# Who writes a block of ones: a memset moved from VectorE to GpSimd at the start of an attention kernel

## The chip, the cores and the metric

The kernel runs on 1 core of one Trainium2 chip. The metric is device time in microseconds (us), the median over the executions. Most executions agree within 0.3%. An execution that is over 1.5% above the fastest of its kernel is classed as slow, and the ratios below use fast executions alone.

## The reference, cut to what matters

```
a   = softmax(phi, axis=seq)                       # 8 batches, 8 heads, 576 tokens, 32 memories
k_m = a^T k ;  v_m = a^T v                         # sums over the tokens
y   = softmax(q k_m^T / 8) v_m                     # attention over the memories
out = ((x @ w_a) * (x @ w_b)) @ w_out              # x: the heads of y side by side
```

The softmax over tokens is never normalised first. The kernel multiplies exp(phi) into k, v and a block of ones beside them; the product with the ones is the denominator. The block holds 1/16 and not 1, which is the scaling that float16 wants here. It is the "fill" of this study. There is one for each of two buffers, and it is written once per buffer.

## The kernel before: the parts that matter

```python
kv_sbs = [consts.tile([P, 3, NHP, NI * D], F16, name=f"kv_sb{t}") for t in range(2)]
#                         ^ plane 0: k, plane 1: v, plane 2: the fill
...
k_f32 = ht[:, 0:2].bitcast(F32)
nc.scalar.dma_start(out=k_f32, in_=rows(k, 0)[:, 0:2])   # half of k, as float32, ScalarE's queue
load_phi(0)                                              # SyncE's queue
load_q(0, halves[0]); load_k(0, halves[1])               # from here GpSimd's queue
load_q(0, halves[1]); load_v(0)
...
make_identity(nc, ident)                                 # GpSimd: a memset and a select
nc.vector.memset(kv_sbs[0][:, 2], 1.0 / CS)              # the fill, L155
nc.vector.tensor_copy(out=kvs[0][:, 0, 0:2], in_=k_f32)  # cast of k, L156
load_wab(0, 256)                                         # weights, GpSimd's queue
ones = ...                  # another tile, not the fill: VectorE memset, two GpSimd selects
load_wab(256, 512); load_wab(512, 1024); load_wab(1024, 1536)
load_wo(0); load_phi(1); ...
nc.gpsimd.memset(kv_sbs[1][:, 2], 1.0 / CS)              # the second buffer's fill, much later
```

TensorE's first real work (L256, "the first sums") reads exp(phi), the cast half of k and the fill. Some 23 us later comes "the last fold" (L337): the product of v_m with the last third of the weights w_b. Both are landmarks below.

## Time and profile before

| | before |
|---|---|
| time, median of 3 | 247.86 us (247.41 to 247.93) |
| span of the profiled execution | 246.2 us |
| first sums start | 7.74 us |
| last fold starts | 30.66 us |
| TensorE busy, over the whole span | 95% |

A busy share of 95% says that TensorE bounds the kernel as a whole. It does not say what bounds the first 30 us. The prediction shows the page's main lines and those of the start. One place it did not look at is the end of the start. Here are the last two folds in the timeline of TensorE (start, duration, engine, line, operation, count, and in brackets the idle time before it and who ended it).

```profile
30.10 0.41 PE L337 MATMUL pva<-wa_sb,kvT 64*32 64x512 f16 x8
...
30.66 0.11 PEld L337 LDWEIGHTS <-kvT 64*32 64x32 f16 x8 [0.45 <-DMA wb_sb<-in_moe_w_b_dram]
30.66 0.41 PE L337 MATMUL pva<-wb_sb,kvT 64*32 64x512 f16 x8 [0.15 <-ACT a_sb L587]
```

The matmul's row has a wait of 0.15 us, and names ScalarE. A reader of that row alone would say that the transfers are no issue. But the weight load that starts with it (PEld) had waited 0.45 us, and for wb: its last part was issued at 14.30 and took 16.3 us to land, so it came near 30.6, just before the fold. TensorE was ready only a little sooner. So already in this profile the stream of loads holds the last fold.

### The profile page before, as it was taken

The page shows a single profiled execution, that of the slowest core. Times are in us where ns is not written, and L with a number is a line of the kernel's source. Part 1 is how long each engine was busy: PE and PEld are TensorE (multiplying, and loading weights), DVE is VectorE, ACT ScalarE, POOL GpSimd, SP SyncE. Part 2 cuts the span into 40 slices and gives each one's busy share as a digit, 9 for nine tenths or more (in the row PEclk, how much of TensorE's full clock was granted, in tenths as well). Part 3 has the DMA queues.
Part 4 walks back from the last instruction along what each step waited for, and adds up shares of the span by engine and source line. Part 5 has one row for each costly group of instructions (what it writes and reads, how often), then busy time and mean ns, then how long its engine had stood idle before and what let it go on. Part 6 is the DMA issues. An engine that isn't in the chain of part 4 may idle for free.

```text
span 246.2 us, 7624 instructions
## 1 busy us (share of the span) xinstructions
PE 233.1 (95%) x3016; PEld 165.7 (67%) x3016; DVE 168.6 (68%) x405; ACT 158.6 (64%) x410; POOL 152.8 (62%) x124
## 2 busy tenths in 40 slices
PE   7589999999998999999999999999999999999992
PEld 2334574456665857777787777877787878888881
DVE  3454784468959968876994559865996586756651
ACT  2364772678697489578856768587856867465430
POOL 8734263499799028892899759892849087946000
PEclk9855999999999999999999999999999999999999
DMA  6999999999969804973159832696120303033253
GB/s 202 209 197 207 209 254 206 256 217 284 225 174 209 165 3 105 235 134 88 27 137 216 184 85 44 160 201 160 35 53 3 85 12 77 19 72 75 45 129 95
DMA packets 26035, 33.81 MB, mean 137 GB/s; under 512 B 1936, under 2 KB 20368, under 8 KB 26000
## 3 DMA queue, kind: packets, MB, share of 16 engines
q0 software_dynamic: 19280, 22.71, 50.5%
q1 hardware_dynamic: 6368, 9.97, 16.3%
q10 hardware_dynamic: 352, 0.66, 0.7%
q8 instruction: 23, 0.38, 0.6%
q14 instruction: 12, 0.10, 0.1%
HBM read 42.47 MB, written 9.44 MB: 211 GB/s over the span
## 4 chain that ended last, share of the span: by engine, by line
PE 89%; DVE 3%; DMA 3%; ACT 2%; issue 1%; DVEq 0%
PE pa L584 21%; PE pb L594 19%; PE py L462 16%; PE pv L462 8%; PE pva L337 6%; PE po L389 5%; PE px L462 4%; DMA phi_sb<-in_phi_dram 3%; PE pkv L213 2%; PE pD L314 2%; PE pscore L292 2%; PE pk L256 2%; PE pT L274 1%; PE pT L242 1%; ACT a_sb L587 1%
## 5 line engine op out<-in xcount | busy, mean ns | idle before, releaser
L597 DVE TENSOR_TENSOR ht<-a_sb,pb 128x288 f16<-128x288 f16 x192 | 83.0, 449 | 41.9 <-ACT a_sb L587 28.7
L587 ACT CAST a_sb<-pa 128x288 f16<-128x288 f32 x192 | 75.0, 406 | 31.6 <-PE pa L584 29.3
L584 PE MATMUL pa<-A,vab 128*128 128x288 f16 x384 | 77.4, 291 | 1.6 <-DVE A L325 1.1
L594 PE MATMUL pb<-A,vab 128*128 128x288 f16 x384 | 77.2, 289 | 0.7 <-ACT vab L349 0.5
L444 POOL TENSOR_TENSOR h_sums<-ht 128x768 f16<-128x768 f16 x28 | 45.8, 1639 | 38.8 <-DVE ht L597 37.3
L594 PEld LDWEIGHTS <-vab 128*128 128x128 f16 x384 | 37.5, 99 | 13.4 <-issue 1.7
L584 PEld LDWEIGHTS <-vab 128*128 128x128 f16 x384 | 34.9, 99 | 16.1 <-issue 8.7
L462 PEld LDWEIGHTS <-h_sums 128*128 128x128 f16 x384 | 37.4, 98 | 6.9 <-issue 0.4
L349 ACT CAST vab<-pva 128x512 f16<-128x512 f32 (+1 forms) x52 | 28.0, 559 | 12.0 <-PE pva L337 12.0
L349 DVE CAST vab<-pva 128x512 f16<-128x512 f32 (+1 forms) x52 | 32.6, 643 | 2.9 <-PE pva L337 2.2
L462 PEld LDWEIGHTS <-ht 128*128 128x128 f16 x288 | 28.1, 98 | 5.6 <-issue 0.4
L462 PE MATMUL py<-w_sums,h_sums 128*128 128x256 f16 x192 | 30.3, 272 | 0.0
L444 POOL TENSOR_TENSOR h_sums<-h_sums,ht 128x768 f16<-128x768 f16 x14 | 23.1, 1647 | 1.0
L444 POOL TENSOR_TENSOR h_sums<-ht,h_sums 128x768 f16<-128x768 f16 x14 | 23.0, 1640 | 1.0
L305 ACT ACTIVATE E<-pscore 128x288 f16<-128x288 f32 x32 | 11.4, 417 | 11.3 <-PE pscore L292 11.2
L325 POOL TENSOR_TENSOR A<-E,R 128x576 f16<-128x576 f16 x10 | 12.8, 1275 | 7.1 <-ACT R L323 6.8
L462 PE MATMUL py<-wo_sb,ht 128*128 128x256 f16 x96 | 16.0, 273 | 0.0
L462 PE MATMUL pv<-w_sums,h_sums 128*128 128x256 f16 x96 | 16.0, 272 | 0.0
L469 ACT ACTIVATE u<-py 128x256 f32<-128x256 f32 x32 | 12.4, 387 | 5.2 <-PE py L462 5.0
L462 PE MATMUL py<-w_sums,ht 128*128 128x256 f16 x96 | 15.5, 272 | 0.1
L462 PE MATMUL px<-wo_sb,ht 128*128 128x256 f16 x96 | 15.4, 273 | 0.0
L204 DVE STREAM_TRANSPOSE qT<-q_sb 128x288 f32<-128x288 f32 x32 | 14.3, 462 | 0.6 <-DMA q_sb<-in_q_dram 0.6
(62 smaller groups left out, 262.7 us busy)
## 6 DMA issues: line engine op xcount, KB each, us to landing
out_dram<-o_sb SPq DMA_DIRECT2D x70, 128.0 KB, 2.6
kv_sb<-in_v_dram POOLq DMA_DIRECT2D x7, 576.0 KB, 10.4
phi_sb<-in_phi_dram POOLq DMA_DIRECT2D x7, 576.0 KB, 4.7
kv_sb<-in_k_dram POOLq DMA_DIRECT2D x7, 576.0 KB, 8.2
q_sb<-in_q_dram POOLq DMA_DIRECT2D x6, 576.0 KB, 13.4
wo_sb<-in_moe_w_out_dram POOLq DMA_DIRECT2D x3, 512.0 KB, 16.3
q_sb<-in_q_dram POOLq DMA_DIRECT2D x4, 288.0 KB, 12.6
wa_sb<-in_moe_w_a_dram POOLq DMA_DIRECT2D x2, 512.0 KB, 14.9
```

The costliest lines, as they stand in the source:

```text
L204: nc.vector.transpose(out=t["qT"][:, hp, :].bitcast(F32), in_=qs[b][:, hp, :].bitcast(F32))
L325: engine.tensor_tensor(out=attn[b][:, g, sl], in0=t["E"][:, g, sl], in1=t["R", g][:, sl], op=ALU.mult)
L337: nc.tensor.matmul(t["pva", lo, z][g][0][32 * j:32 * j + 32, 0:hi - lo], t["kvT"][64 * r:64 * r + 64, 4 + g, M * j:M * j + M], w_sbs[z][64 ...
L349: engine_copy(out=vabs[b][z][:, g, lo:hi], in_=pva[:, 0:hi - lo])
L389: nc.tensor.matmul(po, ht[:, i, P * c:P * (c + 1)], wo_sb[:, i, :], start=(i == 0), stop=(i == NFF - 1))
L444: engine.tensor_tensor(out=out, in0=in0, in1=in1, op=op)
L462: nc.tensor.matmul(po, lhs[:, i], rhs[:, i], start=first and i == 0, stop=i == KH - 1, skip_group_check=not first)
L469: nc.scalar.mul(out=x, in_=po, mul=scale)
L584: nc.tensor.matmul(pa, vab[0][:, g, fs], A[:, g, HALF * hf:HALF * (hf + 1)], start=(g == 0), stop=(g == 1))
L587: nc.scalar.copy(out=a_sb, in_=pa)
L594: nc.tensor.matmul(pb, vab[1][:, g, fs], A[:, g, HALF * hf:HALF * (hf + 1)], start=(g == 0), stop=(g == 1))
L597: nc.vector.tensor_tensor(out=ht[:, i, t0:t0 + HALF], in0=a_sbs[hf - hfs[0]], in1=pb, op=ALU.mult)
```

## The change

The fill goes to GpSimd. It stays in its place in program order, which on GpSimd is behind the first four loads and the identity, and ahead of the weight loads. The intent is to take 2 us from VectorE at the start.

```diff
     make_identity(nc, ident)
-    nc.vector.memset(kv_sbs[0][:, 2], 1.0 / CS)
+    nc.gpsimd.memset(kv_sbs[0][:, 2], 1.0 / CS)
     nc.vector.tensor_copy(out=kvs[0][:, 0, 0:2], in_=k_f32)
     load_wab(0, 256)
```

> **What bounds the kernel now.** I read the page from the top: the busy table, then the clock row, then the chain of work that ended last.
>
> ```profile
> PE 233.1 (95%) x3016; PEld 165.7 (67%) x3016; DVE 168.6 (68%) x405; ACT 158.6 (64%) x410; POOL 152.8 (62%) x124
> PEclk9855999999999999999999999999999999999999
> PE 89%; DVE 3%; DMA 3%; ACT 2%; issue 1%; DVEq 0%
> ```
>
> TensorE is the bound over the span of 246.2 us: 95% busy and 89% of the chain. The clock row dips in slices 2 to 4 only, so the start is the one stage where TensorE waits for others and runs slowly. The change touches only the start. I therefore took the chain of waits for the first 10 us (columns: start in us, duration, what).
>
> ```profile
> 0.81 6.17 DMA phi_sb<-in_phi_dram
> 6.98 0.02 issue
> 7.00 0.69 ACT exp_sb L195
> 7.70 0.04 issue
> 7.74 0.71 PE pk L256 x36
> ```
>
> The start hangs on one transfer. phi of batch 0, issued by SyncE at 0.81, lands at 6.98; ScalarE's exponential follows; the first real matmuls start at 7.74. Those matmuls (the sums of k and of the ones for one half of the heads) also read the fill of ones, so 7.74 is the deadline that matters for the fill. No memset is on the chain. The timeline of the first 8 us shows who is busy before the deadline (start, duration, engine, line, operation, output and input, count, idle before it and its releaser).
>
> ```profile
> 1.32 0.89 POOL L90 DMA_DIRECT2D q_sb<-in_q_dram  x1 [0.80 <-POOLq L699]
> 1.63 1.98 DVE L155 MEMSET kv_sb<- 128x2304 f16 x1 [0.43 <-issue]
> 2.20 0.72 POOL L82 DMA_DIRECT2D kv_sb<-in_k_dram  x1
> ...
> 3.63 0.77 POOL L85 DMA_DIRECT2D kv_sb<-in_v_dram  x1
> ...
> 4.68 0.29 POOL masks.py:199 TENSOR_SCALAR_AFFINE_SELECT ident<-ident 128x128 f16<-128x128 f16 x1
> 4.93 0.77 POOL L99 DMA_DIRECT2D wa_sb<-in_moe_w_a_dram  x1
> ...
> 6.63 0.76 DVE L156 CAST kv_sb<-ht 128x1152 f16<-128x1152 f32 x1 [3.02 <-DMA ht<-in_k_dram]
> ```
>
> VectorE finishes the fill at 3.61 and then stands idle for 3.02 us until k lands; so taking the fill from it buys nothing by itself. GpSimd is free of its four issues and of the identity at 4.97, and from there it queues the weight loads.
>
> **What the Trainium skill says.** On the page "SBUF — State Buffer", section "Who interferes with whom", a VectorE instruction with at most one SBUF input and outside the two-port modes does not contend with GpSimd; copies and casts in SBUF can enter a two-port mode, and then whichever of the two engines starts first holds the shared ports and the other blocks fully. The first half agrees with the trace as far as the issue rows tell: the issues at 2.20 and 3.63, beside the memset, took 0.72 and 0.77, like the 0.77 of the one at 4.93, which has no VectorE work beside it. That two such operations can block each other at all also shows here: the product of E and R (two SBUF inputs) took 1480 ns at 73.63 beside a GpSimd sum that reads SBUF, against a median of 459 ns.
>
> "DMA: Bandwidth & Descriptors", section "SWDGE vs HWDGE vs iDMA", says that GpSimd writes its descriptors into rings in SBUF while loads from SyncE and ScalarE do not use that path, and that the two kinds feed different queues between which a DMA engine takes turns. The queue view of 0.5 us windows (packets, MB, share of 16 engines) shows the first GpSimd packets surprisingly late:
>
> ```profile
> q10 hardware_dynamic: 60, 0.14, 69.8%
> q1 hardware_dynamic: 58, 0.07, 37.0%
> ...
> q1 hardware_dynamic: 100, 0.11, 62.2%
> q10 hardware_dynamic: 43, 0.08, 39.5%
> q0 software_dynamic: 3, 0.00, 4.0%
> ```
>
> Above is 4.5 to 5.0, below 5.0 to 5.5. The first packet of q0, GpSimd's queue, comes about 5.4, 4.1 us after the first issue at 1.32. At 125.81, where the queue was empty, it took about 1.3 us. Either the two hardware queues, which fill the engines (37.0 + 69.8% = 107%), hold q0 back, or the descriptors come late. This is the doubtful point of the case; I return to it under the rivals.
>
> "TensorE: Matmul & The Clock Gate", Part 1, puts the clock down to activity in free-running windows of 3413 ns. The trace agrees in kind: the windows view has a granted clock of 1.00 over 7 to 10 us, 0.56 over 10 to 17, 0.54 over 17 to 25, and 1.00 after that.
>
> **The change part by part.** Removed: one VectorE memset of 1.98 us. Value on the path: 0, because what follows it on VectorE waited 3.02 us for a transfer.
>
> Added: one GpSimd memset of the same 128x2304 f16. The kernel has exactly this instruction already, for the second buffer, and its row says 2.04 us at 34.26. It stands behind the identity, so it runs from 4.68 + 0.29 = 4.97 to 4.97 + 2.04 = 7.01. The first reader started at 7.74 and was released at 7.70. Slack: 7.70 - 7.01 = 0.69 us. Path cost: 0.
>
> Moved: everything that GpSimd does later. The loads of wa and wb for columns 0 to 256 go from 4.93 and 5.68 to about 6.97 and 7.72. The two selects that make the block of ones go from 7.61 to about 8.5 and end near 9.1, while the denominators, their reader, begin at 12.91: 3.8 us of slack. The next four weight loads, 0.75 each, go from 8.25-11.23 to about 9.1-12.2; the load after them had waited until 11.48 for q and now issues about 12.2, and the next one waits for v at 14.30 as before. There the delay has been absorbed.
>
> Do later issues make later data? Only if the queue runs dry. The first four loads bring 288 + 288 + 288 + 576 KB, 1.47 MB, at some 0.2 MB/us from 5.4 on: the queue has its own work until 5.4 + 7.4 = about 12.8 (v lands at 3.63 + 10.4 = 14.0), and the packets indeed turn small, as the weights' are, near 12.5 (224 packets in the 12th us, 360 in the 13th). The weights must be queued by then; issued at 6.97 they have five microseconds in hand. So weights land unchanged. Path cost: 0.
>
> Contention, the one term that is not zero. The VectorE cast of k, at 6.63, is an SBUF-to-SBUF copy: 1152 elements in 761 ns is 1.5 elements/ns, well above one per cycle of a 0.96 GHz engine (clock from "VectorE: DVE Perf Modes", "Specifications"), so it very likely runs in a two-port mode. The new memset still holds the ports until 7.01. If the lock applies to a memset, which only writes, the cast waits 7.01 - 6.63 = 0.38 us and ends at 7.39 + 0.38 = 7.77 and not 7.39. The matmuls need it too and would start about 0.04 us later, near 7.81, and not at 7.74: +0.07 us. Add up to 0.05 us if TensorE now has to pass one more semaphore. Sum: 0 + 0 + 0 + 0.07 + some 0.03 = +0.1 us, an estimate from these rows, and it reaches the end undiminished at most, since TensorE is the bound nearly throughout.
>
> **The rivals.** (1) The old memset did hold up GpSimd's descriptors, in spite of the rule. For it: q0 starts 4.1 us after its issue and not 1.3, and only after the memset is over. Then q0 would start perhaps 2 us sooner, near 3.4, while the transfers of phi and k fill the engines. Early q is worth nothing, as q is not on the chain; phi is. Some 0.9 MB of phi and k are outstanding at 3.4; if q0 takes a third of the engines, an arithmetic estimate is up to 0.9/0.39 x 0.5 = 1.2 us later, more likely 0.5 to 1. Result about 248.3 to 248.9. Against it: the issue rows show no lengthening, and full engines explain the wait as well. I give it 20%.
>
> (2) The fill is late: GpSimd memsets or the four issues take longer beside each other, and TensorE waits on the fill. It would have to lose over 0.69 us; the row at 34.26 ran beside VectorE work and the issues have no reason to slow. It would make +0.3 us or so. 10%.
>
> (3) It helps: GpSimd not writing weight descriptors from 4.93 to 6.4 frees phi and k, or the freed VectorE lets something start sooner. Nothing on the chain waits for that; -0.2 us at best. 10%.
>
> (4) The clock: a shift of the matmuls against the activity windows may move the dip by a window of 3.4 us; at half clock that might be worth up to about 1 us either way, although the three runs of before, whose phases need not agree, lie within 0.52 us.
>
> **Range and chances.** 247.86 + 0.1 = 247.96, say 248.0 us. Downwards, rivals 3 and 4 and the scatter (247.41 to 247.93) give 247.2; upwards, rivals 1 and 4 give 248.8. A 2% change is 5 us, which none of the terms or rivals comes near: faster 0.01, same 0.98, slower 0.01.
>
> **What would show it.** Right: the memset on GpSimd's timeline at about 4.97 for 2.0 us; phi landing still at about 7.0; q0's first packets still near 5.4; the first weight load issued near 7.0 but the fold's first matmuls not later than some 0.1 us; the cast of k ending near 7.8 (lock) or 7.4 (none). Wrong: q0's packets from about 3.4 and phi landing well after 7 (rival 1); the first sums released by the GpSimd memset (rival 2); a clock dip of another length (rival 4). A time under 246 or over 250 would mean a mechanism that I have not seen.

## The result, and the profile after

| | before | after |
|---|---|---|
| time, median of 4 | 247.90 us (247.41 to 247.94) | 247.84 us (247.59 to 248.32) |
| ratio of fast runs | | 1.0007, 95% interval 0.9993 to 1.0021 |
| span of the profiled execution | 246.2 us | 245.8 us |
| first sums start | 7.74 us | 7.71 us |
| last fold starts | 30.66 us | 30.29 us |

A ratio is the mean time of one kernel's fast runs over that of the other's of the same rounds, so it is not quite the ratio of the medians. The verdict is: the same. The interval, some -0.2 to +0.5 us, holds both zero and the predicted +0.1 us.

The timeline of the changed kernel between 4 and 10 us, in the same columns:

```profile
4.93 2.01 POOL L155 MEMSET kv_sb<- 128x2304 f16 x1
...
6.57 0.99 DVE L156 CAST kv_sb<-ht 128x1152 f16<-128x1152 f32 x1 [5.37 <-DMA ht<-in_k_dram]
6.89 0.97 POOL L99 DMA_DIRECT2D wa_sb<-in_moe_w_a_dram  x1
6.93 1.26 ACT L195 ACTIVATE exp_sb<-phi_sb 128x576 f16<-128x576 f32 x2 [4.31 <-DMA phi_sb<-in_phi_dram]
...
7.71 0.68 PE L256 MATMUL pk<-kv_sb,exp_sb 64*32 64x128 f16 x36 [0.88 <-DVE ones L160]
```

The fill runs from 4.93 to 6.94. VectorE's idle time ahead of the cast grows from 3.02 to 5.37 us: the freed time went straight into waiting for k. The cast takes 0.99 and not 0.76, and the first weight load is issued at 6.89 and not 4.93; beside the cast its issue takes 0.97 and not 0.77. The first sums still start 0.78 us after the exponential (6.93 to 7.71), against 0.74 before (7.00 to 7.74).

GpSimd's queue, q0, still sends its first packets in the window from 5.0 to 5.5 us (packets, MB, share of the engines; 3 packets and 4.0% before):

```profile
q0 software_dynamic: 4, 0.00, 5.3%
```

Two rows of the page look as if the start had changed its nature:

```profile
PEclk9977999999999999999999999999999999999998
...
PE 82%; DMA 11%; DVE 3%; issue 1%; ACT 1%; POOL 1%; DVEq 0%; POOLq 0%
```

The clock dip is shallower, and the chain that ended last is now 11% transfers against 3%. The chain itself (start, duration, what) says why:

```profile
3.63 10.32 DMA kv_sb<-in_v_dram
13.94 0.28 issue
14.23 16.02 DMA wb_sb<-in_moe_w_b_dram
30.24 0.04 issue
30.29 0.41 PE pva L337 x8
```

In this execution TensorE was quicker through the start (its fold before the last began at 28.90, against 30.10) and stood waiting at the last fold, 0.97 us by its timeline row, until the last part of wb had landed at 30.24. In the kernel before wb landed near 30.6 and the fold followed at once too. The chain of the page followed the matmul's row there, and so ScalarE: the step from 3% to 11% is a near-tie that fell the other way, and no change in the start's nature. From the last fold to the end the two profiles take the same time: 246.2 - 30.66 = 215.5 us before and 245.8 - 30.29 = 215.5 us after. So the 0.4 us between the spans lies wholly before the last fold, and a floor that no memset moves lies there too. The experiments test this, and whether the clock had anything to do with the change.

### The profile page after: what moved, and what is told of

It reads as the page before. It is cut to its first block, busy times and chain, and to the rows that moved or that the text cites. A ratio compares the mean times of both kernels' runs of the same rounds, so it can differ in the third digit from the quotient of the medians.

```text
span 245.8 us, 7625 instructions
## 1 busy us (share of the span) xinstructions
PE 232.0 (94%) x3016; PEld 165.2 (67%) x3016; DVE 166.6 (68%) x404; ACT 158.6 (64%) x410; POOL 155.2 (63%) x125
## 4 chain that ended last, share of the span: by engine, by line
PE 82%; DMA 11%; DVE 3%; issue 1%; ACT 1%; POOL 1%; DVEq 0%; POOLq 0%
PE pa L584 19%; PE pb L594 18%; PE py L462 16%; PE pv L462 8%; DMA wb_sb<-in_moe_w_b_dram 7%; PE pva L337 5%; PE po L389 5%; DMA kv_sb<-in_v_dram 4%; PE px L462 4%; PE pkv L213 2%; PE pD L314 2%; PE pscore L292 1%; PE pT L242 1%; PE pk L256 1%; POOL q_sb L90 1%
## 5 line engine op out<-in xcount | busy, mean ns | idle before, releaser
L462 PE MATMUL py<-w_sums,h_sums 128*128 128x256 f16 x192 | 30.3, 272 | 0.0
```

Source lines behind the costliest of these rows:

```text
L462: nc.tensor.matmul(po, lhs[:, i], rhs[:, i], start=first and i == 0, stop=i == KH - 1, skip_group_check=not first)
```

## The experiments

**Theory.** Two things bound the start and are nearly tied: TensorE's own chain from phi on, and GpSimd's stream of loads, whose last needed part lands near 30.25. The fill is on neither. **Rivals.** (S) The start is one serial chain, and any delay of the first sums reaches the end. (W) The weights, now issued 2 us later, are a cost that something else happened to pay for. (D) The old fill delayed GpSimd's descriptors. (C) The shorter clock dip is an effect of the change.

All kernels below are the changed kernel with one edit, or none (fill_late_nr has two). All passed the comparison with the reference; one of them computes something wrong on purpose and says so.

### The changed kernel again, twice

No edit.

> The changed kernel once more, unaltered, to size a difference far below one per cent. My theory: the fill is off the path before and after, so the ratio to the kernel before lies within 0.998 to 1.002. Rival (the shorter clock dip of the changed kernel's profile, 0.76 and 0.79 against 0.56 and 0.54, was caused by the change): the clock would be higher again and the time lower, ratio about 0.998 or less. Theory of chance: the clock in this run falls as it likes and says nothing.

> The changed kernel again, unaltered, for the share of long executions: so far 1 in 9 of it, none in 22 of the kernel before. If the change itself made them likelier I expect one or more in five again; if the change leaves the start where it was (first sums at 7.71 against 7.74), about as many as in the kernel before, so likely none. Fast runs: ratio 0.998 to 1.002.

Measured: ratios 1.0004 (0.9991 to 1.0017) and 1.0005 (0.9991 to 1.0019), medians 247.72 and 247.71. Rival C falls. The first four digits of the clock row are 9977 in the changed kernel's first profile and 9995 in the second repeat's. Over the first four runs of the changed kernel the mean granted clock was 0.983, 0.975, 0.972 and 0.982 at 247.59, 247.77, 247.90 and 248.32 us: it varies in one and the same kernel, and the time does not follow it. The kernel before itself ran at 0.967 to 0.999 in the 19 executions of it whose clock the experiments list.

In the first repeat one execution in five took 253.21 us, and it was the profiled one. In the second none did. Over all its runs the changed kernel had one such execution in 14, the kernel before none in 23. That is too few to tell them apart, and the first sums of that long execution began at 7.71 as in the fast ones. What happens in it is told below.

### The fill ahead of the identity

```diff
+    nc.gpsimd.memset(kv_sbs[0][:, 2], 1.0 / CS)
     make_identity(nc, ident)
-    nc.gpsimd.memset(kv_sbs[0][:, 2], 1.0 / CS)
```

> The fill on GpSimd stands ahead of the identity and not behind it, so it ends about 6.4, before the cast of k starts at 6.6. If the cast's 0.99 us (0.76 before) came from the overlap with the fill, it is 0.76 again; if it came from another cause (GpSimd's next issues, or no memset having run on VectorE ahead of it), it stays near 0.99. The first sums begin at 7.7 in both cases, since the exponential of phi releases them; time same, ratio 0.998 to 1.002.

Measured: ratio 1.0001 (0.9988 to 1.0014). Its timeline:

```profile
6.62 0.76 DVE L156 CAST kv_sb<-ht 128x1152 f16<-128x1152 f32 x1 [5.42 <-DMA ht<-in_k_dram]
6.65 0.89 POOL masks.py:199 TENSOR_SCALAR_AFFINE_SELECT ident<-ident 128x128 f16<-128x128 f16 x1
```

The cast is back at 0.76, so the 0.23 us came from the overlap with the fill. The select of the identity now overlaps the cast, begins 0.03 us after it, and pays instead: 0.89 against 0.29. Whichever comes second waits.

### The fill late, over the whole cast

```diff
-    nc.gpsimd.memset(kv_sbs[0][:, 2], 1.0 / CS)
     nc.vector.tensor_copy(out=kvs[0][:, 0, 0:2], in_=k_f32)
     load_wab(0, 256)
+    nc.gpsimd.memset(kv_sbs[0][:, 2], 1.0 / CS)
```

> The fill stands behind the first two weight loads: from about 6.4 to 8.45, over the whole of the cast of k, which can start at 6.6. If GpSimd's write holds the ports for the whole instruction, the cast ends near 9.1 (its row 2.5 us) and the sums begin then, 1.4 us late. If the two share (in the changed kernel 0.37 us of overlap cost 0.23 us), the row is about 1.5 to 2 us and the sums begin with the end of the fill, near 8.5. Time: up by less than the delay of the first sums, since part of it is used up by the wait for the last weights; ratio 1.001 to 1.006.

Measured: 247.87 once, and 253.65, 253.84 and 254.20. The three are classed as slow, so no ratio of fast runs was formed. The port question is answered in its sister kernel fill_late_nr (below), which has the same start:

```profile
6.43 2.06 POOL L157 MEMSET kv_sb<- 128x2304 f16 x1
6.54 2.57 DVE L155 CAST kv_sb<-ht 128x1152 f16<-128x1152 f32 x1 [5.33 <-DMA ht<-in_k_dram]
...
9.25 0.68 PE L256 MATMUL pk<-kv_sb,exp_sb 64*32 64x128 f16 x36 [1.82 <-DVE ones L160]
```

The fill ends at 8.49, and the cast only at 9.11, which is 0.62 us later, most of its own 0.76. So it did next to nothing while the memset ran: the block is complete, not a share. The changed kernel has the same 0.62 us between the two ends (6.94 and 7.56), and so have, to 0.01 us, all nine profiles in which a fill overlaps the cast, whether it stands beside it for 0.30 us or for 1.95. Only about 0.14 us of the cast's 0.76 is ever done before the fill has ended. The expected 2.5 us for this reading was right. The first sums begin 1.5 us late, and one execution still reached 247.87. The expected ratio can't be checked, and three long executions in four were not expected.

### The fill done twice

```diff
     nc.gpsimd.memset(kv_sbs[0][:, 2], 1.0 / CS)
+    nc.gpsimd.memset(kv_sbs[0][:, 2], 1.0 / CS)
```

> The GpSimd fill is done twice in a row, so it ends near 9 (4.93 + 2 x 2.01 = 8.95, or up to 0.6 later if the cast of k takes the ports between the two). The first sums begin then and not at 7.7: the start is 1.25 to 1.9 us later. Theory of two near-tied bounds (the TensorE chain from phi, and the stream of weights whose last part lands near 30.25 whatever the fill does): all but some 0.4 to 1 us of TensorE's lead over the stream is used up first, so the time rises by 0.3 to 1.5 us (ratio 1.001 to 1.006). Rival (purely serial): it rises by the full 1.25 to 1.9. Rival (slack everywhere): no rise. The last third of wb lands near 30.25 in all cases.

Measured: fast runs 247.80 and 248.01, ratio 1.0012 (0.9989 to 1.0034); two executions at 254.43 and 254.46. The timeline of a fast one:

```profile
7.01 2.51 POOL L156 MEMSET kv_sb<- 128x2304 f16 x1
...
9.58 0.68 PE L257 MATMUL pk<-kv_sb,exp_sb 64*32 64x128 f16 x36 [2.75 <-POOL kv_sb L156]
```

Here the fill is the releaser of the first sums, 1.87 us later than in the changed kernel. Yet the last fold begins at 30.52, against 30.29, and the span is 246.1, against 245.8. Rival S, which asks for +1.87, falls for this execution. The fold before the last began at 29.98, against 28.90: 1.08 of the 1.87 us were still there. Of these, all but 0.23 went into the wait that TensorE had anyway: the weight load of the last fold waited 0.43 us for wb, against 1.27. How the other 0.8 us were made up before that, the run does not split; the granted clock over 10 to 29 us was 0.82 in both profiles. The two long executions are counted below.

### The weights issued later still

One spare fill (weights_3us) or three (weights_7us) of the second buffer ahead of the weight loads; the other tile, `ones`, moves up.

```diff
+    ones = ...                                      # moved up from below load_wab(0, 256)
+    for _ in range(1):                              # range(3) in weights_7us
+        nc.gpsimd.memset(kv_sbs[1][:, 2], 1.0 / CS)
     load_wab(0, 256)
```

> Between the fill and the weight loads GpSimd builds the block of ones and fills the second buffer once too often, so the first weight load is issued near 10.4 and not at 6.9 (4.93 before). My claim: the queue has its own work until about 12.8, so nothing changes: first weights used near 16.6, last part of wb lands near 30.25, ratio 0.999 to 1.002. Rival (every us of later issue is a us of later weights): wb's last part near 33.5 and the time up 3 us.

> As the run before, with three spare fills: first weight load near 14.5, 7.5 us later than in the changed kernel. My claim: now the queue runs dry at about 12.8 and starts again about 1.3 us after the issue, near 15.8, so the stream is 2.5 to 3 us later: wb's last part lands near 33 and the time rises by 2.3 to 3 us (ratio 1.009 to 1.012). Rival (the weights aren't a bound at all, TensorE alone is): up by the wait for the first weights only, under 1.5 us.

Measured: with the first weight load issued at 10.36 (weights_3us), the ratio is 1.0003 (0.9985 to 1.0022). With it at 14.52, it is 1.0176 (1.0159 to 1.0194), all four executions fast: +4.4 us. Two folds in the timeline of the second:

```profile
18.44 0.41 PE L339 MATMUL pva<-wa_sb,kvT 64*32 64x256 f16 x8 [3.09 <-DMA wa_sb<-in_moe_w_a_dram]
...
34.26 0.41 PE L339 MATMUL pva<-wb_sb,kvT 64*32 64x512 f16 x8 [1.44 <-DMA wb_sb<-in_moe_w_b_dram]
```

In that run q0 sent 28 packets between 13 and 14 us (360 in the kernel before) and none at all from 14 to 16; in the other the stream had no gap. So the queue does carry its own work to about 13, and rival W falls for a shift of 2 us: a shift of 5.4 us still costs nothing. The size was underestimated (2.3 to 3 expected, 4.4 measured): the last fold came 3.8 us later than with one spare fill (34.26 against 30.43). The dry time itself, from about 13 to about 16, is what was expected. What was not is that q0 did not go on at its old rate: between 19 and 20 us it moved 0.09 MB, against 0.20 with one spare fill. Why is not shown. The rest, 249.9 - 34.26 = 215.6, is as ever.

### The fill on ScalarE

```diff
-    nc.gpsimd.memset(kv_sbs[0][:, 2], 1.0 / CS)
+    col = consts.tile([P, 1], F16, name="col")
+    nc.vector.memset(col, 1.0 / CS)
+    nc.scalar.copy(out=kv_sbs[0][:, 2]..., in_=col.to_broadcast([P, NHP * NI * D]))
```

> The fill is a copy of one column on ScalarE, about 2 us from 2.6 to 4.8, where ScalarE waits for phi. GpSimd's later issues go back to their times of before (weights from 4.93) and the cast has no fill beside it. My theory: cast 0.76, wb of the last third lands near 30.2 as in both kernels, time the same as before and after (ratio 0.998 to 1.002). Rival: if the later issues of the weights cost or gained something in the changed kernel, this one differs from it by that.

Measured: ratio 1.0002 (0.9988 to 1.0015); the copy ran from 2.65 for 2.11 us, the cast took 0.76, the weights were issued from 4.94 as before the change. A third engine for the fill, and again no difference. In its profile phi landed 0.3 us later than in the others and the first sums began at 8.00, so that landmark scatters by this much of itself.

### The fill ahead of the four loads

```diff
     load_phi(0)
     halves = [slice(0, 2), slice(2, 4)]
+    nc.gpsimd.memset(kv_sbs[0][:, 2], 1.0 / CS)
     load_q(0, halves[0])
```

> The fill on GpSimd stands ahead of its first four issues, which start near 3.3 and not 1.3. Two readings of why the GpSimd queue's first packets come only at 5.4: (a) the queues of phi and k fill the engines till then: the first packets stay at 5.4, v lands at 14 and the time is the same (within 0.3 us); (b) the descriptors take about 4 us from the first issue: first packets at 7.4, v lands 2 us later near 16, the last part of wb near 32.2, and the time is 1.5 to 2 us longer (ratio 1.006 to 1.008). In between if the empty-queue figure of 1.3 us from an issue holds: first packets at 5.4 still.

Measured: ratio 1.0008 (0.9995 to 1.0022). The first load is issued 1.44 us later than before, as the timeline has it, and the first packets of q0 come in the same window, 5.0 to 5.5:

```profile
2.76 0.89 POOL L90 DMA_DIRECT2D q_sb<-in_q_dram  x1
```

```profile
q0 software_dynamic: 5, 0.01, 6.6%
```

So the time of the first packets does not follow the issue. Rival D falls twice: without any VectorE memset the packets come no sooner (the changed kernel), and with a later issue no later.

### Half of one early load left out (wrong result on purpose)

```diff
-    nc.scalar.dma_start(out=k_f32, in_=rows(k, 0)[:, 0:2])
+    nc.scalar.dma_start(out=k_f32[:, 0:1], in_=rows(k, 0)[:, 0:1])
...
-    nc.vector.tensor_copy(out=kvs[0][:, 0, 0:2], in_=k_f32)
+    for c in range(2):
+        nc.vector.tensor_copy(out=kvs[0][:, 0, c:c + 1], in_=k_f32[:, 0:1])
```

> Wrong result on purpose: only the first half of what ScalarE loads of k is loaded, and is cast twice, so the two queues of phi and k carry a quarter less (about 0.89 MB for 1.18 MB). If those queues hold back GpSimd's queue, its first packets come about 0.7 us sooner, near 4.6, and phi lands near 6.2; v and the last part of wb land some 0.7 us sooner (wb near 29.5). With both bounds of the start sooner by 0.7 the time falls by 0.4 to 0.8 us (ratio 0.997 to 0.9985). If the descriptors take 4 us by themselves, the first packets stay at 5.4.

Measured (the comparison did not notice the wrong half of k in one of eight batches): the first packet falls in the window 4.0 to 4.5, and 31 in the next, 4.5 to 5.0, where the kernel before and the changed one had none:

```profile
q0 software_dynamic: 1, 0.00, 1.3%
```

```profile
q0 software_dynamic: 31, 0.04, 58.2%
```

The early hardware queues are what holds q0 back: GpSimd's four issues stand at the same times as in the changed kernel (1.32 to 3.63), and only those queues have less to carry. phi landed so early that the exponential began at 5.42, yet the first sums began only at 7.30, and now the fill is what releases them:

```profile
7.30 0.68 PE L257 MATMUL pk<-kv_sb,exp_sb 64*32 64x128 f16 x36 [0.44 <-POOL kv_sb L155]
```

The fast runs gain little: ratio 0.9983 (0.9964 to 1.0002), with one slow execution at 251.99. The last fold waited 0.98 us for wb and began at 30.12, not at the 29.5 that I expected: v landed 0.4 us sooner (9.91 us after its issue, against 10.32), the last part of wb only 0.2. So phi came 1.5 us sooner, but the first sums only 0.41, since they now waited for the fill, and the last fold waited for wb again. This agrees with the theory of the two bounds but does not test it: rival S asks for 0.4 us here, and the ratio is 0.4 us.

### The long executions: one product off VectorE

Six executions took 253 to 254.5 us: one of the changed kernel, three of fill_late and two of fill_twice. No difference of the change rests on them. But far more of them come with a late fill: in fill_late and fill_twice, whose first sums come 1.5 to 1.9 us late, five executions of eight were long, against one of 37 of the changed kernel and the kernel before. The median of all four executions of fill_twice is 251.22, which the ratio of its fast runs hides. Two of the six were profiled, and both show one thing that no fast profile shows. First a fast execution of the changed kernel, then the long one:

```profile
48.06 0.45 DVE L325 TENSOR_TENSOR A<-E,R 128x576 f16<-128x576 f16 x1
...
49.29 3.11 POOL L429 TENSOR_TENSOR w_sums<-wo_sb 128x1536 f16<-128x1536 f16 x1
```

```profile
49.25 4.24 DVE L325 TENSOR_TENSOR A<-E,R 128x576 f16<-128x576 f16 x1
...
50.06 3.10 POOL L429 TENSOR_TENSOR w_sums<-wo_sb 128x1536 f16<-128x1536 f16 x1
...
53.88 0.41 PE L584 MATMUL pa<-A,vab 128*128 128x288 f16 x1 [2.78 <-DVE vab L349]
```

GpSimd starts its sums of weights when its loads let it, at 49.29 and 50.06 here. VectorE's product comes when TensorE's chain lets it. Where it was done by 48.51, before GpSimd's sums, it took 0.45 us; where it came 1.2 us later it took 4.24, longer than the first of those sums, and TensorE stood still for 2.78. In that long execution the last fold had begun at 31.48, about 1.2 us late; in fill_late's at 31.97. In the nine fast profiles counted further below it began between 30.12 and 30.66. In both long ones wb had landed well before (near 30.1 and 30.3), so that TensorE's own chain was the later bound; and from the last fold to the end they take 220.0 and 219.9 us, against 215.5.

One thing does not fit: alone, the product would have ended 0.36 us before the row of GpSimd's sums begins. Between them stands a load issue of GpSimd, from 49.30 to 50.05. But beside such issues the product takes its usual time elsewhere (0.46 us at 70.57 in the kernel before, all of it within an issue). To test the collision, I tried to take it away:

```diff
-        engine = nc.vector if b < 3 else nc.gpsimd
+        engine = nc.vector if b < 3 and (b, g) != (1, 1) else nc.gpsimd
```

> fill_late had three executions in four near 253.8; its profile has one product of E and R on VectorE (batch 1, second half, L325) at 4.24 us and not 0.46, beside GpSimd's sums of weights (L429, read SBUF). Here that product alone goes to GpSimd, where it stands ahead of those sums and can't run beside them; the late fill stays. Theory of the collision: no execution above 250, the time within 1.5 us of the kernel before. Rival (the long executions are the clock's doing, or the late start's own): half or more of the executions stay near 253.8.

> The same move of one product to GpSimd in the changed kernel with its fill in place. The product takes about 1.27 us on GpSimd and not 0.46, in a place where TensorE has other work for about 1 us: time the same as before within 1 us (ratio 0.998 to 1.004), and no execution above 250. If the move costs more than the collision's absence is worth, the median is over 248.5.

Measured: fill_late_nr 249.77 to 252.49 (six executions), ratio 1.0137 (1.0092 to 1.0183); after_nr 249.03 to 251.74, ratio 1.0098 (1.0055 to 1.0141). Nothing stayed near 253.8, but both misses are plain: seven of the twelve are over 250, and the edit itself costs 2 us. On GpSimd the product took 1.27 us and stood ahead of the loads of the next batch but one and of the sums of weights, which began at 52.83 and not at 49.29. And in the profiled execution of after_nr the collision has moved and not gone: two products of the next batch, at 71.01 and 74.32, took 1.17 and 2.50 us beside GpSimd's sums of h, where the changed kernel has 0.46 (70.20) and 1.47 (73.26), and TensorE stood still for 1.86 us at 76.87 and not for 1.06. The edit changed more than the collision, so it proves little. That the collision makes the long executions is what two profiles show at the place, not what a clean removal has shown. It stays open, and so does the 251.99 us execution of k_half, which was not profiled.

## Why the prediction was right, point by point

The forecast of 248.0 against a median of 247.84 is inside the scatter of the executions. That the two are so near says nothing for the term of +0.1 us; what follows checks the terms by the traces.

**Removed from VectorE, worth 0.** Right: the idle time ahead of the cast grew from 3.02 to 5.37 us.

**Added to GpSimd, hidden with 0.69 us to spare.** Right: 4.93 to 6.94 measured, 4.97 to 7.01 predicted; only where phi came sooner (k_half) or the fill was doubled did TensorE wait for it by name. Rival 2 fell.

**Moved issues, no cost.** Right, and with more room than needed: 2 us later in the change, 5.4 us later in weights_3us, both free; 9.6 us later costs 4.4. The predicted absorption at the issue that waits for v came as told (14.23 against 14.30).

**Contention of the cast, +0.07 us.** Right in kind. The block is real and complete (2.57 us in fill_late_nr). The size was a little large: the cast ended at 7.56 and not 7.77, since the fill ended 0.07 us sooner than worked out and the cast needed 0.62 us after it and not 0.76. The first sums came 0.04 us later against the exponential, released by VectorE. In the second repeat, where phi landed later, the exponential released them and nothing was lost (7.03 to 7.76). The ratios 1.0007, 1.0004 and 1.0005 (0.1 to 0.2 us) do not exclude zero.

**Rival 1, descriptors held up by the old memset (20%).** It did not come true, as fill_first and k_half show; its alternative, that the queues of phi and k fill the engines, is what they found.

**Rival 3, a gain from later weight issues.** It did not come: fill_act issues the weights at 4.94 again and times the same.

**Rival 4, the clock.** It does move from execution to execution, and the scatter is the size that was allowed for; it is not the change's doing. The prediction's "agrees in kind" says too much: over 10 to 25 us the clock was about 0.55 while TensorE was busy for 13.15 of the 15 us, so its figures show that the clock dips, and not that activity sets it.

**What the prediction missed,** without harm to its number: it took the chain from phi for the only bound of the start, and let a delay of it reach the end "undiminished at most, since TensorE is the bound nearly throughout". The stream of loads is a second bound, nearly tied. In nine fast profiles (before, after, fill_early, fill_act, fill_first, fill_twice, weights_3us, the second repeat, k_half) the first sums begin anywhere from 7.30 to 9.58 us, while the last fold begins between 30.12 and 30.66, and the rest of the span is 215.5 to 215.6 us in each. The last part of wb lands between 29.7 and 30.6, and in eight of the nine the weight load of the last fold waits for it; in the second repeat TensorE's own chain sets it (wb landed near 29.7, the fold began at 30.47). So a step of the sum that was off by some tenths would mostly have been lost in that wait; and the executions scatter by more than that anyway.

## What to carry to other kernels

Before moving work off an engine, read what that engine does next: if it waits for a transfer, the freed time becomes waiting and nothing else. A start that hangs on one chain in one profile may have a second bound just behind it; compare the landmark at its end, not at its beginning, over several executions, and read the row of the weight load beside that of its matmul. And a memset on GpSimd is not free for a VectorE copy beside it: put it where VectorE has nothing to cast.

## What the Trainium skill lacked or had wrong

- "DMA: Bandwidth & Descriptors", section "SWDGE vs HWDGE vs iDMA", has a DMA engine take turns between the queues. While two hardware queues filled the engines, GpSimd's queue got next to nothing: first packets in the window from 5.0 to 5.5 us, whether the first issue stood at 1.32 or 2.76 us, and in that from 4.0 to 4.5 when the hardware queues had a quarter less to carry. No page says that early hardware loads can hold back GpSimd's.
- "SBUF — State Buffer", section "Who interferes with whom": complete blocking agrees (a cast of 0.76 us took 2.57 beside a 2.06 us memset, a select of 0.29 took 0.89 beside a cast). It could add that a cast that is blocked has done a little already: it ended 0.61 to 0.62 us after the memset's end in nine profiles, whatever the overlap, and takes 0.76 alone.
- The same section infers that a product with two SBUF inputs is not held by descriptor generation. The fast profiles agree: in the kernel before the product at 70.57, within a load issue that ran from 70.11 to 70.90, took 0.46 us as elsewhere. What stays open is the long execution shown: there the product's row began at 49.25, beside an issue from 49.30 to 50.05, and had not ended when GpSimd's sums began at 50.06. Rows on GpSimd are rough and no run was made for this.
